# A last store in column pieces over all 128 rows, in a fused attention and GEGLU kernel

## The chip, the cores and the metric

The kernel runs on one core of a Trainium2 chip. The metric is the time of one execution on the device in microseconds; the figure for a kernel is the median of its runs. Traces come from one profiled execution, and times inside it count from the start of its span.

## What is computed

Squared-ReLU attention without a softmax, whose heads are joined to token rows, followed by a gated feed-forward block. The inputs are float32; `q`, `k` and `v` have the shape (8, 12, 448, 64), and the output has 3584 rows (8 batches of 448 tokens) of 768 columns.

```python
scores = scale * np.matmul(q, k.transpose(0, 1, 3, 2))     # scale = 1 / sqrt(64)
attn = np.maximum(scores, 0.0) ** 2 / S                    # S = 448
x = np.matmul(attn, v)                                     # heads joined: (3584, 768)
g = x @ w_gate                                             # (3584, 1536)
gelu = 0.5 * g * (1.0 + erf(g * inv_sqrt2))
val = x @ w_val
return (gelu * val @ w_out).astype(np.float32)             # (3584, 768)
```

## The kernel before

**Layout of the tokens.** The 448 tokens of a batch are seen as 64 positions times 7 chunks (P = 64, SC = 7): token 7p + c is position p of chunk c. A chunk is thus every seventh row of the output, and two neighbouring chunks lie one row apart. In DRAM a row of the output has 768 float32, 3072 bytes; two positions of one chunk are 7 rows apart.

**Stages.** Queries, keys and values are loaded and turned to bfloat16 by GpSimd's transfers, transposed, multiplied on TensorE as 64 by 64 blocks, passed through ReLU on ScalarE (line 740) and squared on VectorE (line 749). The value products give xT, the gate and value products with GELU give uT, and the output product makes rows of 768 columns. All matmuls go through the helper at line 406.

**The output product.** Tokens are taken in 14 groups (gr = 0 to 13, the last is FINAL) of four chunks. A group is two tiles, t0 and t1, of two chunks each, 128 rows with one chunk on partitions 0 to 63 and the next on 64 to 127 (HALF names the two halves). In the last group these are chunks 3 and 4, and 5 and 6, of the last batch. The product of a group is formed by seven smaller products, named 1 to 7 and taken in the order of CHAIN = "1726453". Each gives a 128 by 384 block (OGS = 384), the left or the right half of the columns of t0 or t1; some are added to a block already there. So each tile has its left and right half finished at different times, and the very last product is "3", the right half of t0.

**Around the change.** In `add_product`, `emit_read` (lines 1226 to 1232) takes a finished block out of PSUM into the tile `osb` in SBUF: a copy by ScalarE or VectorE (line 1231), or an addition by VectorE (line 1229). For the last group's "3" the copy is ScalarE's alone (`rd.other = None`). `emit_store` (lines 1247 to 1250) stores one half of the partitions, 64 rows of one chunk, as one transfer. A finished tile is usually stored by two such transfers of 192 KB over whole rows, on SP's queue; in the last two groups the second goes to ScalarE's queue. Tile t0 of the last group is the exception: its left and right columns are stored separately, each by two transfers of 96 KB, one half of the partitions on SP's queue and the other on ScalarE's. In every plain load and store, the 64 or 128 partitions are the outermost count of the transfer on both sides (lines 447, 456, 469, 485, 1250).

**Order of the work.** The kernel is written as operations with an engine, an estimated cost, dependencies and a priority (`Op`). `run_plan` emits them one after another in the order of a planned timetable: it takes at each step the operation that can start first, and at equal times the one with the lower `prio`. The order of the later TensorE units is a list written out by hand (LINE). The order of emission is each engine's program order; the waits between engines follow from what the instructions read and write. At the end of the program (line 1513) SP waits for the landing of every transfer, and the engines meet once more.

Of the kernel before, what the change touches and what calls it, by code (L numbers as in the profile page):

```python
# [316 lines left out]
def kernel(  # L317
# [10 lines left out]
    nc = tc.nc  # L328
# [5 lines left out]
    B, H, S, D = q.shape  # L334
    P = 64
    SC = S // P
# [13 lines left out]
    OGS = d_model // NG  # L350
# [62 lines left out]
    ACT, DVE, POOL, SP, IDLE = [], [], [], [], []  # L413
# [687 lines left out]
    sums, osb, stored = {}, {}, {}  # L1101
# [58 lines left out]
    def add_product(at, gr, name, final):  # L1160
# [4 lines left out]
        t0, t1 = 2 * gr, 2 * gr + 1  # L1165
        chunks = st["chunks"]
# [6 lines left out]
        box = st["box", stage]  # L1173
# [13 lines left out]
        else:  # L1187
            t, half = source
# [4 lines left out]
        def emit(r, fc):  # L1193
# [4 lines left out]
            for j in range(2):  # L1198
# [15 lines left out]
                for fc in range(KH)] for r in range(2)]  # L1214
        st["last", name] = ops[1][-1]
        left, right = slice(0, OGS), slice(OGS, 2 * OGS)
        t, cols, added = {"1": (t0, left, False), "2": (t0, left, True), "3": (t0, right, False),
                          "6": (t1, left, False), "4": (t1, left, True),
                          "7": (t1, right, False), "5": (t1, right, True)}[name]

        def osb_of(t):
            if t not in osb:
                osb[t] = opool.tile([TT, d_model], f32, name="osb", tag="osb")
            return osb[t]

        def emit_read(copy=nc.scalar.copy):
            o = osb_of(t)[:, cols]
            if added:
                ins = nc.vector.tensor_tensor(o, box[0][:, 0:OGS], o, op=ALU.add)
            else:  # L1230
                ins = copy(o, box[0][:, 0:OGS])  # L1231
            rd.ins = ins.ins

        engine = "DVE" if added else "ACT"
        before = {"2": "1", "4": "6", "5": "7"}.get(name)
        rd = Op(engine, 0.52 if added else 0.45, emit_read,
                [ops[1][-1], *([st["read", before]] if before else ())], lag=0.2, prio=0,
                other=None if added else ("DVE", 0.52, lambda: emit_read(nc.vector.tensor_copy)))
        if not added:
            rd.takes = osb_ring, lambda: stored[t][-1] if t in stored else None, t  # L1240
        reads = [rd]
        if final and name == "3":
            rd.other = None
        (DVE if added else ACT).append(rd)
        st["read", name] = rd
        st["read", stage] = rd
        def emit_store(j, engine=nc.sync, part=slice(0, d_model)):
            b, c = chunks[t % 2][j]
            rows = out[b * S:(b + 1) * S, :].rearrange("(p c) d -> c p d", c=SC)
            engine.dma_start(rows[c, :, part], osb[t][HALF[j], part])  # L1250

        if name in "2345":
            st["done", t] = [*st.get(("done", t), ()), *reads]
            if final and t == t0:
                SP.append(Op("SP", 0.6, lambda: emit_store(0, nc.sync, cols), reads, prio=-1))
                ACT.append(Op("ACT", 0.5, lambda: emit_store(1, nc.scalar, cols), reads, prio=-1))
                SP[-1].stored = ACT[-1].stored = 0.25
            elif len(st["done", t]) == 2:
                queues = (SP, "SP", 0.6, nc.sync), (ACT, "ACT", 0.5, nc.scalar)
                stored[t] = []  # L1260
                for j in range(2):
                    pool, name_, cost, engine = queues[j if gr >= FINAL - 1 else 0]
                    op = Op(name_, cost, lambda j=j, engine=engine: emit_store(j, engine), st["done", t],
                            lag=2.5, prio=-1)
                    op.stored = 0.5
                    stored[t].append(op)
                    pool.append(op)
# [83 lines left out]
    for gr in range(FINAL + 1):  # L1351
        work += [(LATER, 5, add_product, (gr, x, gr == FINAL)) for x in CHAIN]
# [47 lines left out]
    for kind, lo, hi in pairs:  # L1400
        if kind == "with":
            upper.append((tau[place[lo]], hi))
        else:
# [8 lines left out]
            t = tau[min(behind + 1, len(PE0))]  # L1412
# [47 lines left out]
    for u in later:  # L1460
        if u.name[0] == "o":
            b = u.name[1]
# [55 lines left out]
```

## Time and profile before

| | us |
|---|---|
| median of 3 runs | 403.87 (403.24 to 403.89) |
| the profiled execution, its own time | 404.06 |
| its span, first to last instruction | 402.3 |
| granted TensorE clock, mean | 0.996 |
| ScalarE busy (61%) | 243.6 |
| DMA traffic of the queues | 44.38 MB |

The span is what the trace can explain; the execution has some 1.8 us around it. Engines have short names in the rows: PE is TensorE's matmul, PEld its weight load, DVE VectorE, ACT ScalarE, POOL GpSimd, SP SyncE. A name with a q (SPq, ACTq) is the engine's sequencer: it issues transfers and waits, which is not counted as busy. Of DMA, the share is the mean busy share of the core's 16 DMA engines; q1 is the queue on which SP issues, q10 that of ScalarE, q0 that of GpSimd. A transfer is listed as issued, with its size and the time from issue to landing. In a row of instructions, `128x384 f32<-128x384 f32` is the output's and the input's shape, `x34` the count, and behind the bar stand busy microseconds and the mean nanoseconds of one.

### The profile page before, as it was taken

The page shows a single profiled execution, that of the slowest core. Times are in us where ns is not written, and L with a number is a line of the kernel's source. Part 1 is how long each engine was busy: PE and PEld are TensorE (multiplying, and loading weights), DVE is VectorE, ACT ScalarE, POOL GpSimd, SP SyncE. Part 2 cuts the span into 40 slices and gives each one's busy share as a digit, 9 for nine tenths or more (in the row PEclk, how much of TensorE's full clock was granted, in tenths as well). Part 3 has the DMA queues.
Part 4 walks back from the last instruction along what each step waited for, and adds up shares of the span by engine and source line. Part 5 has one row for each costly group of instructions (what it writes and reads, how often), then busy time and mean ns, then how long its engine had stood idle before and what let it go on. Part 6 is the DMA issues. An engine that isn't in the chain of part 4 may idle for free.

```text
span 402.3 us, 18625 instructions
## 1 busy us (share of the span) xinstructions
PE 393.5 (98%) x8510; PEld 339.5 (84%) x8510; DVE 301.5 (75%) x518; ACT 243.6 (61%) x362; POOL 76.8 (19%) x124
## 2 busy tenths in 40 slices
PE   8999999999999999999999999999999999999994
PEld 3555888888999979999999989768998899998884
DVE  2886886558878877898998787779888875786642
ACT  4957777376677667766767666556766535353130
POOL 6548323160320402101210303010110000000000
PEclk9999999999999999999999999999999999999998
DMA  7999999699696886755758988463542320000244
GB/s 104 175 185 165 196 197 155 95 161 151 100 216 91 141 196 91 112 68 86 89 97 190 162 132 124 95 108 51 57 56 70 95 68 4 2 3 3 58 125 137
DMA packets 75022, 44.38 MB, mean 110 GB/s; under 512 B 34368, under 2 KB 71488, under 8 KB 74944
## 3 DMA queue, kind: packets, MB, share of 16 engines
q0 software_dynamic: 38752, 24.39, 44.7%
q1 hardware_dynamic: 35792, 18.03, 22.2%
q8 instruction: 66, 1.08, 1.1%
q10 hardware_dynamic: 400, 0.79, 0.6%
q14 instruction: 12, 0.10, 0.1%
HBM read 48.76 MB, written 11.01 MB: 149 GB/s over the span
## 4 chain that ended last, share of the span: by engine, by line
PE 98%; issue 1%; ACT 0%; DVE 0%
PE ff L406 85%; PE sp L406 9%; PE ff L594 1%; PE sp L673 1%; PE ff L1425 1%; PE ff L673 1%; PE ff L636 0%; ACT attnT L740 0%; ACT qkT L644 0%; ACT osb L1231 0%; DVE held L392 0%; DVE table L395 0%; ACT xT L822 0%
## 5 line engine op out<-in xcount | busy, mean ns | idle before, releaser
L406 PE MATMUL ff<-xT,wg 64*64 64x448 bf16 x1872 | 189.6, 349 | 0.5 <-issue 0.5
L740 ACT ACTIVATE attnT<-sp 128x896 bf16<-128x896 f32 x168 | 151.3, 921 | 54.1 <-PE sp L406 46.0
L406 PE MATMUL ff<-xT,wv 64*64 64x448 bf16 x1440 | 153.1, 349 | 0.5 <-issue 0.5
L406 PEld LDWEIGHTS <-wv 64*64 64x64 bf16 x1872 | 111.1, 106 | 13.2 <-issue 2.3
L406 PEld LDWEIGHTS <-wg 64*64 64x64 bf16 x1872 | 110.7, 106 | 10.8 <-issue 0.4
L749 DVE TENSOR_TENSOR attnT<-attnT 128x1792 bf16<-128x1792 bf16 (+1 forms) x98 | 92.3, 954 | 10.9 <-ACT attnT L740 10.5
L406 PE MATMUL ff<-attnT,v 64*64 64x448 bf16 (+1 forms) x768 | 84.8, 326 | 0.3 <-issue 0.2
L406 PEld LDWEIGHTS <-s 64*64 64x64 bf16 x1344 | 77.3, 107 | 4.2 <-issue 0.2
L406 PE MATMUL sp<-qkT 64*64 64x448 bf16 (+1 forms) x768 | 79.3, 328 | 1.0 <-ACT qkT L644 0.6
L406 PE MATMUL ff<-wo,s 64*64 64x384 bf16 x672 | 59.6, 323 | 0.0
L406 PEld LDWEIGHTS <-uT 64*64 64x64 bf16 x912 | 54.8, 107 | 2.4
L1039 DVE TENSOR_TENSOR uT<-gel,ff 128x448 bf16<-128x448 bf16 x60 | 37.1, 619 | 21.9 <-PE ff L406 19.4
L406 PE MATMUL ff<-wt,s 64*64 64x384 bf16 x672 | 52.8, 322 | 0.0
L406 PEld LDWEIGHTS <-v 64*64 64x64 bf16 x768 | 47.4, 107 | 4.7 <-issue 1.5
L406 PE MATMUL ff<-ts,ws 64*64 64x448 bf16 x432 | 50.0, 349 | 0.0
L406 PE MATMUL ff<-ts,wv 64*64 64x448 bf16 x432 | 49.6, 349 | 0.0
L483 POOL DMA_DIRECT2D v<-in_v_dram x48 | 29.7, 632 | 89.1 <-ACT attnT L740 49.2
L406 PE MATMUL ff<-wo,uT 64*64 64x384 bf16 x576 | 46.4, 322 | 0.0
L406 PEld LDWEIGHTS <-qkT 64*64 64x64 bf16 x768 | 38.6, 106 | 8.5 <-issue 4.4
L1034 ACT ACTIVATE gel<-ff 128x448 bf16<-128x448 f32 x60 | 32.7, 546 | 21.1 <-PE ff L406 20.7
L406 PEld LDWEIGHTS <-ws 64*64 64x64 bf16 x648 | 39.8, 106 | 3.2
L956 DVE TENSOR_TENSOR part<-ff,part 128x448 f32<-128x448 f32 x54 | 32.6, 622 | 8.2 <-PE ff L406 6.0
(60 smaller groups left out, 381.8 us busy)
## 6 DMA issues: line engine op xcount, KB each, us to landing
out_dram<-osb SPq DMA_DIRECT2D x51, 192.0 KB, 3.4
v<-in_v_dram POOLq DMA_DIRECT2D x48, 128.0 KB, 5.0
qk<-in_q_dram POOLq DMA_DIRECT2D x23, 224.0 KB, 4.9
qk<-in_k_dram POOLq DMA_DIRECT2D x23, 224.0 KB, 5.5
wg<-in_moe_w_gate_dram POOLq DMA_DIRECT2D x6, 384.0 KB, 8.6
wv<-in_moe_w_val_dram POOLq DMA_DIRECT2D x6, 384.0 KB, 9.8
wo<-in_moe_w_out_dram POOLq DMA_DIRECT2D x8, 288.0 KB, 9.3
out_dram<-osb ACTq DMA_DIRECT2D x3, 192.0 KB, 3.3
```

The source lines that it names most:

```text
L406: return nc.tensor.matmul(o, lhsT, rhs, start=start, stop=stop, skip_group_check=onto, tile_position=(P * row, P * col))
L483: return nc.gpsimd.dma_start(v16[b, m][HALF[i], :, :, :], v[b, h0:h1].rearrange("h (p c) d -> p h c d", c=SC)[:, :, c0:c0 + VC, :])
L594: nc.tensor.matmul(t[:, :], warm[:, 0:128], warm[:, :], start=True, stop=True)
L673: nc.tensor.transpose(t[HALF[j], c, :], src[:, 2 * r + j, c, :], ident[:, :], tile_position=(0, P * j))
L740: relu.ins = nc.scalar.activation(duo["a"][:, u % 2, :, :], box[0][:, :, 0:S], AF.Relu).ins
L749: nc.vector.tensor_tensor(a[:, part], a[:, part], a[:, part], op=ALU.mult)
L956: rd.ins = nc.vector.tensor_tensor(t[:, :], box[0][:, 0:S], t[:, :], op=ALU.add).ins
L1034: nc.scalar.activation(gel[b, fc][:, :], box[0][:, 0:S], AF.Gelu)
L1039: u_op[b, fc].ins = nc.vector.tensor_tensor(uT[b][:, fc, :], gel.pop((b, fc))[:, :], box[0][:, 0:S], op=ALU.mult).ins
L1425: nc.tensor.matmul(t[HALF[j], :], warm[:, HALF[j]], warm[:, :], start=True, stop=True, tile_position=(0, P * j))
```

## The change

It touches product "3" of the last group, the right half of t0. Its copy of 384 columns by ScalarE becomes two copies of 192 columns, one after the other. Each piece is stored by one transfer over all 128 rows: the first on SP's queue, waiting for the first copy, the second on ScalarE's queue, waiting for the second. Before, the two transfers waited for the whole copy and each took 64 rows of all 384 columns. The DRAM side of the new transfers is `rows[c:c + 2]`, a view with two chunks, 64 positions and 192 columns; the SBUF side is 128 partitions by 192 columns. The planner's costs of the copies are 0.32 each.

```diff
         if final and name == "3":
-            rd.other = None
+            half = OGS // 2
+            copies = []
+
+            def emit_piece(h):
+                part = slice(OGS + h * half, OGS + (h + 1) * half)
+                ins = nc.scalar.copy(osb_of(t)[:, part], box[0][:, h * half:(h + 1) * half])
+                copies.append(ins)
+                if h == 0:
+                    rd.ins = ins.ins
+                return ins
+
+            rd.other, rd.cost, rd.emit = None, 0.32, lambda: emit_piece(0)
+            reads.append(Op("ACT", 0.32, lambda: emit_piece(1), [rd], lag=0.2, prio=-2))
+            reads[1].after = rd
+            ACT.append(reads[1])
+
+        def emit_wide(h, engine):
+            part = slice(OGS + h * OGS // 2, OGS + (h + 1) * OGS // 2)
+            (b, c), (b_, c_) = chunks[t % 2]
+            assert b == b_ and c_ == c + 1
+            rows = out[b * S:(b + 1) * S, part].rearrange("(p c) d -> c p d", c=SC)
+            engine.dma_start(rows[c:c + 2], osb[t][:, part])
...
-            if final and t == t0:
+            if final and t == t0 and name == "3":
+                SP.append(Op("SP", 0.6, lambda: emit_wide(0, nc.sync), [rd], prio=-1))
+                ACT.append(Op("ACT", 0.5, lambda: emit_wide(1, nc.scalar), [reads[1]], prio=-1))
+                SP[-1].stored = ACT[-1].stored = 0.25
+            elif final and t == t0:
                 SP.append(Op("SP", 0.6, lambda: emit_store(0, nc.sync, cols), reads, prio=-1))
```

## The prediction, made before the change was run

> **What bounds the kernel now.** I read the page first, then the chain of work that ended last over the final microseconds, then the instructions, the transfers and SP's waits after the last matmul.
>
> ```profile
> span 402.3 us, 18625 instructions
> PE 393.5 (98%) x8510; PEld 339.5 (84%) x8510; DVE 301.5 (75%) x518; ACT 243.6 (61%) x362; POOL 76.8 (19%) x124
> ```
>
> TensorE is busy for 98% of the span, so only two things can move the time: TensorE's own work, or what remains to be done when it has finished. The diff leaves the matmuls alone. The chain over 390 to 403 us shows where they end:
>
> ```profile
> 389.99 7.27 PE ff L406 x157
> 397.25 0.02 issue
> 397.27 0.48 ACT osb L1231
> ```
>
> The last matmul ends at 397.25, and ScalarE's copy of the last product runs to 397.75. The span ends at 402.3, so the **tail** is 5.05 us, and 4.5 us of it lie behind the copy. The last issue in ScalarE's timeline, and the transfers issued between 397.2 and 398.4 with their microseconds to landing, fill it:
>
> ```profile
> 397.78 0.50 ACTq L1250 DMA_DIRECT2D out_dram<-osb  x1
> ...
> out_dram<-osb ACTq DMA_DIRECT2D x1, 192.0 KB, 3.8
> out_dram<-osb SPq DMA_DIRECT2D x1, 96.0 KB, 3.1
> out_dram<-osb ACTq DMA_DIRECT2D x1, 96.0 KB, 3.3
> ```
>
> Two 96 KB stores are issued at 397.78, one on SP's queue and one on ScalarE's. They land 3.1 and 3.3 us later, the last at about 401.06. From there to 402.3 the program only closes (1.24 us): SP's waits on line 1513.
>
> ```profile
> SPq L1513 <- DMA out_dram<-osb: 2.6, 2, 2.3
> ```
>
> So the landing of the very last store sets the end. How the 3.3 us are spent is read from the busy share of the 16 DMA engines; the last two columns are that share and GB/s:
>
> ```profile
> 397.75:398.25 0.50, 0.00 (x0) 0.00 (x0) 0.00 (x0) 0.00 (x1) 0.00 (x0) 1.00 0.82 264
> 398.25:398.75 0.50, 0.00 (x0) 0.00 (x0) 0.00 (x0) 0.00 (x0) 0.00 (x0) 1.00 0.99 344
> 398.75:399.25 0.50, 0.00 (x0) 0.00 (x0) 0.00 (x0) 0.00 (x0) 0.00 (x0) 0.75 0.96 326
> 399.25:399.75 0.50, 0.00 (x0) 0.00 (x0) 0.00 (x0) 0.00 (x0) 0.00 (x0) 0.50 0.89 295
> 399.75:400.25 0.50, 0.00 (x0) 0.00 (x0) 0.00 (x0) 0.00 (x0) 0.00 (x0) 0.50 0.92 335
> 400.25:400.75 0.50, 0.00 (x0) 0.00 (x0) 0.00 (x0) 0.00 (x0) 0.00 (x0) 0.50 0.12 40
> ```
>
> All 16 engines are nearly full until 400.25, on stores of the preceding products and then on these two. The 0.12 in the last row is 0.06 us per engine, so an engine ends on average at 400.31. The landing at 401.06 comes 0.75 us later: part is the slowest engine's lag, part the way home. The tail is therefore bound by **DMA engine time**, and what the change does to that decides.
>
> **The change, part by part.** *The copies.* One copy of 384 columns becomes two of 192, a shape that the trace does not have. The copies of 384 and 448 columns, by form, are nearest, and the pair of copies at 389.29 shows how two follow each other:
>
> ```profile
> L952 ACT COPY part<-ff 128x448 f32<-128x448 f32 x35 | 18.5, 533 | 18.6 <-PE ff L406 16.1 <-DVE uT L965 1.8
> L1231 ACT COPY osb<-ff 128x384 f32<-128x384 f32 x34 | 16.2, 479 | 24.6 <-PE ff L406 23.4 <-issue 1.1
> ...
> 389.29 0.86 ACT L1231 COPY osb<-ff 128x384 f32<-128x384 f32 x2 [1.54 <-PE ff L406]
> ```
>
> 64 columns are worth 533 - 479 = 54 ns, so 192 columns less are worth 162, and a piece takes 479 - 162 = 317 ns (nothing saved, 479, is one end; half of it, 240, the other). Two copies took 0.86 us instead of 0.96, so the second starts 0.10 before the first ends. The first piece is done at 397.27 + 0.32 = 397.59, 0.16 earlier than now; the second at 397.59 - 0.10 + 0.32 = 397.81, 0.06 later. SP's store goes out 0.16 earlier and ScalarE's 0.06 later. Behind SP's store only the closing waits are queued, behind ScalarE's only its closing drain; TensorE and VectorE have nothing left. The planner places the new copy after everything else, so nothing ahead of 397.25 moves. Were SP's store held until the second copy too, it would go out at 397.84, which costs it 0.22; with the engines full until 400.25 either start disappears in their backlog.
>
> *The stores.* Before, a transfer carries 64 rows of 1536 bytes; after, 128 rows of 768 bytes. The bytes are the same. What matters is among how many engines the rows are dealt.
>
> ```profile
> q10 hardware_dynamic: 400, 0.79, 0.6%
> ...
> out_dram<-osb ACTq DMA_DIRECT2D x3, 192.0 KB, 3.3
> ...
> out_dram<-osb ACTq DMA_DIRECT2D x2, 96.0 KB, 2.8
> ```
>
> ScalarE's queue, q10, carries exactly five stores, and 400 packets are 80 for each: 64 rows and 16 short ones. I read this as sixteen equal shares of four rows, each with a closing packet. Every plain load and store of this kernel (lines 447, 456, 469, 485 and 1250) has 64 or 128 as the outermost count on both sides, and 16 divides both. The new transfer is the first that has not: in DRAM its rows are `c p d` with c = 2 outermost, p = 64 inside, since the rows of one chunk lie 21.5 KB apart and the two chunks 3 KB apart, so that no single count of 128 describes them. The SBUF side has 128. If the shares are cut along the outermost count, as all shares here can have been, there are **two**: one engine takes the 64 rows of the first chunk, one those of the second, and fourteen do nothing. Both stores are cut alike, so I let both have the same pair. No row shows such a transfer. Sixteen shares would need a cut inside the inner count on one side and in the outer one on the other; nothing in the trace needs that. I take two.
>
> The Trainium skill, page "DMA: Bandwidth & Descriptors", section "Why a DMA increments its semaphore by 16 and not by 1", states the same: the engine count is the largest up to 16 that divides the slowest dimension of both sides, on these queues the lowest-numbered engines. By that rule the count here is 2, and both stores share one pair; the trace's 16 short packets per 64-row store agree, and no run yet shows a smaller count.
>
> *The price of a row.* Two windows hold one whole store of ScalarE's queue each, 389.9 to 390.6 (96 KB) and 395.95 to 396.66 (192 KB); a third, 180.7 to 180.9, only 256-byte packets of the transposing transfers:
>
> ```profile
> q10 hardware_dynamic: 80, 0.10, 41.0%
> ...
> q10 hardware_dynamic: 80, 0.20, 70.5%
> ...
> DMA packets 168, 0.04 MB, mean 215 GB/s; under 512 B 168, under 2 KB 168, under 8 KB 168
> ## 3 DMA queue, kind: packets, MB, share of 16 engines
> q1 hardware_dynamic: 168, 0.04, 106.7%
> ```
>
> Engine time is share x window x 16: 0.410 x 0.70 x 16 = 4.59 us, 72 ns per row of 1536 bytes with the short packets in it; 0.705 x 0.71 x 16 = 8.01 us, 125 ns per row of 3072; 1.067 x 0.20 x 16 / 168 = 20 ns per 256 bytes. On the line from 20 to 72, 768 bytes cost 20 + 52 x 512/1280 = 41 ns; I take 40, as the 72 include the short packets. The ends are 20 and 72.
>
> *The sum.* Now each engine spends 2 x 4.59/16 = 0.57 us on the two stores. With two shares on one pair, each of the two engines has 2 x 64 x 40 ns = 5.12 us of them, 4.55 more. It ends at 400.31 + 4.55 = 404.86. Of the 0.75 us above I keep 0.4 for the way home and drop 0.35 as the lag among sixteen engines, which two hardly have (an estimate); so the last store lands at 405.26 instead of 401.06: **+4.2 us**. The closing 1.24 us stays. The profiled execution took 404.06 us, 402.3 of it span; the median of the runs is 403.87. So I forecast 408.26 for the former and 403.87 + 4.2, rounded, 408.1 for the median. With 20 ns a row the sum is 2.56 - 0.57 - 0.35 = +1.6 (405.5), with 72 it is 9.2 - 0.57 - 0.35 = +8.3 (412.2).
>
> **The rivals.** *Sixteen shares, engines bind: no change.* If the rows are dealt over all engines whatever the outermost count, each has 16 x 40 = 0.64 us instead of 0.57. SP's half starts 0.16 earlier, ScalarE's 0.06 later, and the end moves by between -0.05 and +0.15 us: about 403.9. For it: the bytes are the same and every store so far ran on sixteen. Against it: none of them had a small outermost count. It decides as soon as the engine count does not depend on that count. The Trainium skill, the same page, section "Rules for kernel authors", advises one 128-partition transfer instead of two over disjoint halves, because halves share the same engines anyway; by that advice alone the result is this rival's, and the trace agrees only in that both stores now overlap on full engines.
>
> *Dealt better than feared.* Either sixteen shares with a pace set by the number of rows, or two stores on different pairs. Two stores alone in the window 304.5 to 307.5 show the pace:
>
> ```profile
> DMA  0000000000000007985976948996299695952000
> ```
>
> Busy in 22 of 40 slices of 75 ns, 1.65 us for 128 rows, though two stores of 8.01 us need only 1.0 on sixteen engines. At that pace 128 more rows add up to 1.65 us. Different pairs give 64 x 40 ns = 2.56 - 0.57 - 0.35 = +1.6. Both end near 405.5. Against the first: the engines' shares above leave no room for a slower feeder in the tail; against the second: nothing in the text of the transfers tells one queue's engines from the other's.
>
> *A gain.* If the tail hung on the first store's start, 0.16 us could be won; that is within what a measurement can tell from no change (0.2%, 0.8 us), so faster by more needs something that I cannot name.
>
> **How the numbers follow.** Two shares on one pair 0.75, dealt better 0.10, no change 0.13, faster 0.02. The first two are slower by over 0.2% (0.85), the third is within it. Within the forecast most lies between 406.3 and 410.5, as 72 ns is the price of a row twice as long. The range runs from 405.0, which takes in the second case, to 410.5; outside are no change (0.13), faster (0.02) and a long row's price (about 0.04).
>
> **What would show it.** The same engines' shares, after the last matmul: near 2/16 = 0.12 for some 4 us after 400.3, at 40 GB/s or so, would show two engines; a fall to zero at 400.5 would show sixteen. Packets on q10 should be 64 + 16 for each old store and 128 and some short ones for the new one, 2 short if there are two shares. ScalarE should have one copy more, of 0.32 us, and its store issue near 397.84; SP's wait for the last transfer should grow from 2.3 to about 6.5 us. A landing about 3.3 us after issue would prove the forecast wrong, and so would a change ahead of 397.25.

## The result, and the profile after

The changed kernel takes 408.5 us in the median (407.71 to 409.19), beside 403.56 us for the kernel before (401.56 to 403.89), four runs each. The ratio is 1.0123, with a 95% interval of 1.009 to 1.0156: slower by 1.2%. The profiled execution took 408.88 us, 4.82 more than that of before. From its page come the span and the packets of ScalarE's queue:

```profile
span 407.1 us, 18624 instructions
...
q10 hardware_dynamic: 450, 0.79, 0.6%
```

The queue carried 400 packets before. Four of its five stores are the old ones with 80 packets, 320 in all; so the new one has 130: 128 rows and **two** short packets, where every store of this queue had sixteen. The chain that ended last, over 390 to 408 us, shows that little moved ahead of the stores:

```profile
389.97 7.58 PE ff L406 x161
397.55 0.02 issue
397.57 0.06 ACT osb L1248
397.63 0.16 issue
397.79 0.32 ACT osb L1248
```

The last matmul ends at 397.55, 0.30 later than in the profiled execution of before, and the span ends at 407.1. I call the time from the end of the last matmul to the end of the span the **tail**: 5.04 us before, 9.54 after, by the times of the trace (the rows are rounded). The two copies stand where they were expected. The timelines of ScalarE and of SP go on:

```profile
397.57 0.54 ACT L1248 COPY osb<-ff 128x192 f32<-128x192 f32 x2 [5.58 <-PE ff L406]
398.14 1.21 ACTq L1264 DMA_DIRECT2D out_dram<-osb  x1
```

```profile
397.92 0.62 SPq L1264 DMA_DIRECT2D out_dram<-osb  x1
```

What fills the tail is again read from the stretches of half a microsecond; the last two columns are the busy share of 16 DMA engines and GB/s:

```profile
399.75:400.25 0.50, 0.00 (x0) 0.00 (x0) 0.00 (x0) 0.00 (x0) 0.00 (x0) 0.71 0.39 118
400.25:400.75 0.50, 0.00 (x0) 0.00 (x0) 0.00 (x0) 0.00 (x0) 0.00 (x0) 0.50 0.14 29
400.75:401.25 0.50, 0.00 (x0) 0.00 (x0) 0.00 (x0) 0.00 (x0) 0.00 (x0) 0.50 0.12 29
401.25:401.75 0.50, 0.00 (x0) 0.00 (x0) 0.00 (x0) 0.00 (x0) 0.00 (x0) 0.50 0.11 32
...
402.25:402.75 0.50, 0.00 (x0) 0.00 (x0) 0.00 (x0) 0.00 (x0) 0.00 (x0) 0.50 0.14 46
...
403.75:404.25 0.50, 0.00 (x0) 0.00 (x0) 0.00 (x0) 0.00 (x0) 0.00 (x0) 0.50 0.14 46
404.25:404.75 0.50, 0.00 (x0) 0.00 (x0) 0.00 (x0) 0.00 (x0) 0.00 (x0) 0.50 0.11 37
404.75:405.25 0.50, 0.00 (x0) 0.00 (x0) 0.00 (x0) 0.00 (x0) 0.00 (x0) 0.50 0.07 23
405.25:405.75 0.50, 0.00 (x0) 0.00 (x0) 0.00 (x0) 0.00 (x0) 0.00 (x0) 0.50 0.05 15
```

Before, the share stood at 0.92 until 400.25 and then fell to nothing. Now it drops to 0.14, which is two of sixteen engines (2/16 = 0.125, and packets overlap a little), and stays at 0.11 to 0.14 for more than 4 us; from 404.75 it is 0.07, one engine. At 46 GB/s the pair moves 23 GB/s each, one row of 768 bytes in 33 ns. That pace holds from 402.25 on; in the stretches before it the pair is about as busy but moves only 29 to 41 GB/s, which the experiments come back to. SP's waits at the end of the program are now

```profile
SPq L1538 <- DMA out_dram<-osb: 7.1, 3, 4.5
```

against 2.6 us before. The last store lands at 405.91, and the program closes.

### The profile page after: what moved, and what is told of

It reads as the page before. It is cut to its first block, busy times and chain, and to the rows that moved or that the text cites. A ratio compares the mean times of both kernels' runs of the same rounds, so it can differ in the third digit from the quotient of the medians.

```text
span 407.1 us, 18624 instructions
## 1 busy us (share of the span) xinstructions
PE 391.6 (96%) x8507; PEld 338.5 (83%) x8510; DVE 301.8 (74%) x518; ACT 243.8 (60%) x363; POOL 76.9 (19%) x124
## 4 chain that ended last, share of the span: by engine, by line
PE 93%; DMA 3%; POOL 1%; issue 1%; ACT 0%; SPq 0%; POOLq 0%
PE ff L406 83%; PE sp L406 8%; DMA qk<-in_k_dram 2%; DMA qkT<-qkr 1%; PE sp L673 1%; POOL qk L468 1%; PE ff L594 1%; PE ff L673 1%; ACT attnT L740 0%; ACT osb L1248 0%; POOL ident masks.py:199 0%; POOL ident masks.py:197 0%; SPq L515 0%; ACT xT L822 0%; POOLq L1527 0%
## 5 line engine op out<-in xcount | busy, mean ns | idle before, releaser
L406 PEld LDWEIGHTS <-wg 64*64 64x64 bf16 x1872 | 108.4, 106 | 10.7
L749 DVE TENSOR_TENSOR attnT<-attnT 128x1792 bf16<-128x1792 bf16 (+1 forms) x98 | 92.3, 953 | 10.8 <-ACT attnT L740 10.3
L406 PE MATMUL sp<-qkT 64*64 64x448 bf16 (+1 forms) x768 | 75.9, 328 | 3.0 <-DMA qkT<-qkr 1.7
L406 PEld LDWEIGHTS <-s 64*64 64x64 bf16 x1344 | 74.4, 107 | 4.8 <-issue 0.2
L406 PEld LDWEIGHTS <-uT 64*64 64x64 bf16 x912 | 52.4, 107 | 2.9
L406 PEld LDWEIGHTS <-v 64*64 64x64 bf16 x768 | 46.5, 107 | 5.0 <-issue 1.9
L406 PEld LDWEIGHTS <-qkT 64*64 64x64 bf16 x768 | 36.5, 106 | 10.4 <-issue 3.9
```

Source lines behind the costliest of these rows:

```text
L406: return nc.tensor.matmul(o, lhsT, rhs, start=start, stop=stop, skip_group_check=onto, tile_position=(P * row, P * col))
L749: nc.vector.tensor_tensor(a[:, part], a[:, part], a[:, part], op=ALU.mult)
```

## The experiments

Theory: shares are cut along the outermost count, here 2, and the tail is the time of the engines that get a share. Rivals: short rows (128 rows of 768 bytes are slow wherever they go), copies and issue, the spacing of the rows in DRAM, a fixed delay of such transfers. The time of an execution varies by a few microseconds with where the last matmul ends (395.0 to 398.7 in these profiles, with the same matmuls, but for one kernel that stands still in the middle), so the tail tells more than one run's time. Each tail is that of one profiled execution; where ratios are given they rest on several runs.

**Only the outermost count is changed.** The wide stores go to the rows of the first batch, as N blocks of 128/N neighbouring rows, and the right columns of the last t0 are left unwritten; copies, number of issues, bytes and rows per transfer stay. (In the edit N stands for the number of blocks: the run with N = 2 has `n=2` and `0:64`.)

```diff
-            rows = out[b * S:(b + 1) * S, part].rearrange("(p c) d -> c p d", c=SC)
-            engine.dma_start(rows[c:c + 2], osb[t][:, part])
+            rows = out[0:S, part].rearrange("(n r) d -> n r d", n=N)[:, 0:128 // N, :]
+            engine.dma_start(rows, osb[t][:, part])
```

N = 2:

> The two wide stores go to other rows, in the first batch (stored long before), as 2 blocks of 64 neighbouring rows: outermost count 2 as in the changed kernel, another spacing of the rows. It leaves the right rows of the last product unwritten. The tail is the time from the end of the last matmul to the end of the span: 5.05 us before, 9.5 after. Theory (shares are cut along the outermost count, here 2, and the two engines' time is the tail): tail 9.5 us, 2 completions. Rival 'spacing' (rows 21.5 KB apart in two chunks 3 KB apart collide in memory): the tail falls to 5 to 6 us. Rival 'short rows' (128 rows of 768 bytes are slow whatever the engines): 9.5.

N = 4:

> As blocks2, but 4 blocks of 32 rows, so an outermost count of 4; same rows, bytes, copies and issues. The last product's right rows stay unwritten. Theory: four engines with 2 x 32 rows each, half the time of the pair, so of the 4.5 us lost about 2.4 come back: tail 6.7 to 7.2 us. Rival 'short rows' and rival 'copies and issue' (the second copy and the later issues): 9.5 us.

N = 16:

> As blocks2, but 16 blocks of 8 rows, an outermost count of 16. The last product's right rows stay unwritten. Theory: sixteen engines with 16 rows each, 0.64 us: tail 5.0 to 5.4 us, median within 0.5 us of the kernel before. Rival 'short rows' and rival 'copies and issue': tail 9.5 us, median 408 to 409.

N = 8, after the first three:

> As blocks2, blocks4 and blocks16, with 8 blocks of 16 rows, an outermost count of 8; the last product's right rows stay unwritten. Theory: eight engines with 2 x 16 rows, 1.06 us each: tail 5.4 to 6.2 us if all engines start together; blocks4 (8.97 instead of 6.7 to 7.2) had one engine some 1.65 us behind the three others, and such a laggard would make it 6.5 to 8.

N = 4 once more:

> blocks4 once more (the last product's right rows stay unwritten), since its tail of 8.97 us missed the 6.7 to 7.2 that four equal engines should give, with one engine 1.65 us behind. If the laggard is an accident of one execution: 6.7 to 7.4. If it belongs to the kernel: 8.5 to 9.3, with one late completion again.

The span and the packets of ScalarE's queue, from the pages with N = 2, 4, 8 and 16 in turn:

```profile
span 405.8 us, 18624 instructions
...
q10 hardware_dynamic: 450, 0.79, 0.6%
```

```profile
span 404.5 us, 18624 instructions
...
q10 hardware_dynamic: 452, 0.79, 0.6%
```

```profile
span 404.7 us, 18624 instructions
...
q10 hardware_dynamic: 456, 0.79, 0.6%
```

```profile
span 403.8 us, 18624 instructions
...
q10 hardware_dynamic: 464, 0.79, 0.6%
```

Less 320 for the four old stores and 128 for the rows, these are 2, 4, 8 and 16 short packets: one for each share. The chain has the end of the last matmul, here for N = 2 and then for N = 16; span less this is the tail:

```profile
396.02 0.02 issue
```

```profile
398.75 0.02 issue
```

| N | rows on one engine | at 33 ns | tail, us | over 5.04 |
|---|---|---|---|---|
| 2 | 128 | 4.2 | 9.78 | 4.74 |
| 4 | 64 | 2.1 | 8.97, again 8.78 | 3.93, 3.74 |
| 8 | 32 | 1.1 | 6.34 | 1.30 |
| 16 | 16 | 0.5 | 5.02 | none |

With an outermost count of 16, everything else as in the changed kernel, the loss is gone; the ratio to the kernel before is 0.9993 (0.9956 to 1.003). So it is neither the short rows, nor the copies, nor the number of issues. With N = 2 the rows have another spacing and the loss stays, so the spacing is not it. N = 4 **missed** the 6.7 to 7.2 of equal engines in both executions (the second time within the 8.5 to 9.3 that was named for a lasting laggard), and N = 8, at 6.34, came out between the 5.4 to 6.2 of equal engines and the 6.5 to 8 with a laggard: there is a second term that the number of rows doesn't give. The stretches of N = 4 show where it sits:

```profile
398.50:399.00 0.50, 0.00 (x0) 0.00 (x0) 0.00 (x0) 0.00 (x0) 0.00 (x0) 0.50 0.11 5
...
400.50:401.00 0.50, 0.00 (x0) 0.00 (x0) 0.00 (x0) 0.00 (x0) 0.00 (x0) 0.50 0.21 72
401.00:401.50 0.50, 0.00 (x0) 0.00 (x0) 0.00 (x0) 0.00 (x0) 0.00 (x0) 0.50 0.15 49
401.50:402.00 0.50, 0.00 (x0) 0.00 (x0) 0.00 (x0) 0.00 (x0) 0.00 (x0) 0.50 0.07 23
402.00:402.50 0.50, 0.00 (x0) 0.00 (x0) 0.00 (x0) 0.00 (x0) 0.00 (x0) 0.50 0.07 23
402.50:403.00 0.50, 0.00 (x0) 0.00 (x0) 0.00 (x0) 0.00 (x0) 0.00 (x0) 0.50 0.07 23
```

Three engines are done by about 401.5, and one works on alone (0.07, 23 GB/s) for 1.5 us more. Such a laggard came in both executions: the trace has a completion event for each engine of a store, and the last of the four came 0.77 and 1.65 us after the third for the two stores, and 1.18 and 1.20 the second time. The first row shows something else: early on the busy engines hardly moved anything (5 GB/s).

**The same pieces in transfers of 64 rows.**

```diff
-                SP.append(Op("SP", 0.6, lambda: emit_wide(0, nc.sync), [rd], prio=-1))
-                ACT.append(Op("ACT", 0.5, lambda: emit_wide(1, nc.scalar), [reads[1]], prio=-1))
-                SP[-1].stored = ACT[-1].stored = 0.25
+                for j in range(2):
+                    SP.append(Op("SP", 0.6, lambda j=j: emit_store(j, nc.sync, slice(OGS, OGS + OGS // 2)),
+                                 [rd], prio=-1))
+                    SP[-1].stored = 0.12
+                for j in range(2):
+                    ACT.append(Op("ACT", 0.5, lambda j=j: emit_store(j, nc.scalar, slice(OGS + OGS // 2, 2 * OGS)),
+                                  [reads[1]], prio=-1))
+                    ACT[-1].stored = 0.12
```

> The two column copies stay, but each piece is stored by two transfers of 64 rows (one chunk each), outermost count 64: both of the first piece on SP's queue, both of the second on ScalarE's. Rows of 768 bytes as in the changed kernel, 256 of them. Theory: 16 shares each, tail 5.1 to 5.7 us (the second issue on each queue comes 0.5 us later than a single one), median within 0.8 us of the kernel before. Rival 'short rows': 9.5 us.

Its page has the span, its chain the end of the last matmul:

```profile
span 403.1 us, 18626 instructions
```

```profile
398.13 0.02 issue
```

The tail is 4.98 us, a little under the 5.1 to 5.7 that was expected, the ratio 1.0002 (0.9972 to 1.0031). The 256 rows of 768 bytes are all there, now with the outermost count 64, and cost nothing; nor do two more issues show. This is the column split as such, with its early first piece, and it brings nothing that can be measured.

**The copies alone**, with the stores of before, which wait for both pieces:

```diff
-            if final and t == t0 and name == "3":
-                SP.append(Op("SP", 0.6, lambda: emit_wide(0, nc.sync), [rd], prio=-1))
-                ACT.append(Op("ACT", 0.5, lambda: emit_wide(1, nc.scalar), [reads[1]], prio=-1))
-                SP[-1].stored = ACT[-1].stored = 0.25
-            elif final and t == t0:
+            if final and t == t0:
```

> Only the copy is cut into two column pieces; the stores are the old ones, 64 rows of 384 columns each, waiting for both copies. Theory: the second piece ends 0.06 us later than the one copy did, so the tail (end of the last matmul to end of the span; 5.04 us before) is 5.0 to 5.2 us and the median stays within noise. Rival 'copies and issue': 9 us or more.

The tail was 5.03 us, the ratio 0.999 (0.9961 to 1.0019). The rival of copies and issue is out.

**One wide store and two narrow ones**: the first piece is stored as in the changed kernel, the second by two transfers of 64 rows.

```diff
-                ACT.append(Op("ACT", 0.5, lambda: emit_wide(1, nc.scalar), [reads[1]], prio=-1))
-                SP[-1].stored = ACT[-1].stored = 0.25
+                SP[-1].stored = 0.25
+                for j in range(2):
+                    ACT.append(Op("ACT", 0.5, lambda j=j: emit_store(j, nc.scalar, slice(OGS + OGS // 2, 2 * OGS)),
+                                  [reads[1]], prio=-1))
+                    ACT[-1].stored = 0.12
```

> The first piece is stored as in the changed kernel (128 rows, outermost count 2, SP's queue), the second by two transfers of 64 rows on ScalarE's queue. Theory with the 33 ns per row that the changed kernel shows on one engine: the pair has 64 rows each instead of 128, 2.1 us instead of 4.2, so the tail is 6.9 to 7.6 us. Rival 'a fixed delay': a transfer with a small outermost count is late by a fixed time, whatever its size: 9 to 9.8 us, as with two of them.

The tail was 8.20 us: above the theory, below the fixed delay. The two completions of the wide store came 1.40 us apart; without that gap the tail would be 8.20 - 1.40 = 6.8, near the theory. (The very last landing, 0.18 us later, is one of the sixteen shares of the second 64-row store.) So there is a term for the rows and one for a laggard.

**One copy, one wide store** of 384 columns on SP's queue:

```diff
+        def emit_wide(engine):
+            (b, c), (b_, c_) = chunks[t % 2]
+            rows = out[b * S:(b + 1) * S, cols].rearrange("(p c) d -> c p d", c=SC)
+            engine.dma_start(rows[c:c + 2], osb[t][:, cols])
...
-            if final and t == t0:
+            if final and t == t0 and name == "3":
+                SP.append(Op("SP", 0.6, lambda: emit_wide(nc.sync), reads, prio=-1))
+                SP[-1].stored = 0.5
+            elif final and t == t0:
```

> One copy of 384 columns as before, then one store of all 128 rows (1536 bytes each) on SP's queue, outermost count 2; no transfer on ScalarE's queue for this product. Theory if an engine's time goes with the bytes: 64 rows of 61 to 66 ns on each of two engines, 4.1 us, tail 8.8 to 9.6 us, median 407.5 to 408.5. If it goes with the number of rows (33 ns each whatever the length): 2.1 us, tail 6.9 to 7.6. Rival 'copies and issue' (no second copy, one issue): near 5 us.

The median was 408.44 us, the ratio 1.0162 (1.0126 to 1.0197), the tail 9.62, just past what the theory allows. The stretches:

```profile
400.50:401.00 0.50, 0.00 (x0) 0.00 (x0) 0.00 (x0) 0.00 (x0) 0.00 (x0) 0.50 0.14 52
...
402.50:403.00 0.50, 0.00 (x0) 0.00 (x0) 0.00 (x0) 0.00 (x0) 0.00 (x0) 0.50 0.07 28
403.00:403.50 0.50, 0.00 (x0) 0.00 (x0) 0.00 (x0) 0.00 (x0) 0.00 (x0) 0.50 0.07 25
```

One engine alone moves some 25 GB/s (the last two rows), and its last packets start 61 ns apart, beside 33 for rows of half the length: an engine's time goes with the bytes, and the number of rows hardly matters. With a single issue and the old copy the loss is all there. The completions are 1.06 us apart.

**Is the second engine slow, or hindered?** Two more kernels ask for the laggard. The first stores five tiles in the middle of the kernel (groups 7 to 9) by one transfer of 128 whole rows, and leaves the end as it was:

```diff
+            elif len(st["done", t]) == 2 and gr in (7, 8, 9) and chunks[t % 2][0][0] == chunks[t % 2][1][0]:
+                def emit_wide():
+                    b, c = chunks[t % 2][0]
+                    rows = out[b * S:(b + 1) * S, :].rearrange("(p c) d -> c p d", c=SC)
+                    nc.sync.dma_start(rows[c:c + 2], osb[t][:, :])
+                op = Op("SP", 0.6, emit_wide, st["done", t], lag=2.5, prio=-1)
...
```

> The kernel before, but the tiles of groups 7, 8 and 9 whose two chunks are in one batch are stored by one transfer of 128 whole rows, outermost count 2, on SP's queue, in the middle of the kernel where TensorE has work for long after; the last groups are as before. Theory: two engines, 64 rows of about 121 ns each, so each lands 8.5 to 10 us after its issue instead of 2.7, and the median stays the same, since nothing waits for it. About the second engine, which in the tails of the changed kernel and of one_wide lagged by 1.0 to 1.25 us: if traffic in the tail did that, the two completions come within 0.3 us of each other here; if the second engine is slower by itself, 1 us or more apart.

The first two, issued at 302.30 and 306.78, completed at 312.64 on both engines and at 320.17 and 320.18: no laggard. The other three ended 0.53, 0.40 and 0.41 us apart, between the two answers that were named. Even the first, which had the pair to itself, landed 10.3 us after its issue, not 8.5 to 10. The rest of what was expected **failed**: the median is 414.98 us, the ratio 1.0301 (1.0274 to 1.0328). The waits, and VectorE's timeline, say why:

```profile
PE ff L406 <- DVE osb L1231: 7.1, 1, 7.1
```

```profile
320.27 1.02 DVE L1231 COPY osb<-ff 128x384 f32<-128x384 f32 x2 [7.57 <-DMA out_dram<-osb]
```

The second store stood behind the first on the same two engines and landed 13.4 us after its issue; the copy that needed its `osb` buffer again waited, the product's bank was not freed, and TensorE stood still for 7.1 us. The page of this kernel has

```profile
span 413.3 us, 18619 instructions
PE 397.0 (96%) x8507; PEld 345.2 (84%) x8510; DVE 300.0 (73%) x515; ACT 245.6 (59%) x365; POOL 77.0 (19%) x124
```

Outside its busy time TensorE had 8.8 us before (402.3 - 393.5) and has 16.3 here, 7.5 more; the other 3.5 us of the longer span are more busy time for the same matmuls. The granted clock was down beside the stall (0.74 and 0.58 in the two stretches of 5 us after 315):

```profile
315.00:320.00 5.00, 0.00 (x0) 0.00 (x0) 0.00 (x0) 0.00 (x0) 0.00 (x0) 0.74 0.12 50
320.00:325.00 5.00, 4.12 (x62) 3.10 (x65) 2.49 (x4) 0.48 (x1) 0.00 (x0) 0.58 0.01 3
```

The second kernel takes older stores out of the end. As a measure, first that edit to the kernel before:

```diff
-            if final and t == t0:
+            if gr >= FINAL - 1 and t == t0:
```

> The kernel before, with the first tile of the last group but one (t0 of group 12) stored in column halves too: its left half goes out when product 2 of that group is done, so that only 192 KB instead of 384 KB of it are left for the last two microseconds. By the engine times of the kernel before that takes 2 x (8.01 - 4.59)/16 = 0.43 us of engine time out of the backlog, so the tail would be 4.6 to 5.05 us instead of 5.04 and the median 0 to 0.4 us lower (within what is measurable, or just). If the tail hangs on the way home of the last store alone, nothing changes.

The tail is 4.45 us in its profile, shorter than the 4.6 to 5.05 that was expected, but the median of 12 runs is 402.72 beside 402.55 (ratio 0.9999, 0.9979 to 1.0018): the 0.6 us, 0.15%, could not be told from no change, so no faster kernel is claimed. Then the same edit on the changed kernel:

```diff
-            elif final and t == t0:
+            elif gr >= FINAL - 1 and t == t0:
```

> The changed kernel, with the first tile of the last group but one stored in column halves as in split12, so that 192 KB less of older stores stand before the two wide ones. In the changed kernel the two engines' completions lie 1.25 and 1.02 us apart; in wide_quiet, where nothing else was in flight, 0.00 and 0.01. If the older stores in flight make the second engine late: completions at most 0.7 us apart and a tail of 8.2 to 9.0 us instead of 9.54. If the lag has another cause that goes with the end of the program: 1.0 to 1.3 us apart, tail 9.0 to 9.5 us (the 0.6 us that split12 won on sixteen engines may come off).

```profile
401.00:401.50 0.50, 0.00 (x0) 0.00 (x0) 0.00 (x0) 0.00 (x0) 0.00 (x0) 0.50 0.14 46
401.50:402.00 0.50, 0.00 (x0) 0.00 (x0) 0.00 (x0) 0.00 (x0) 0.00 (x0) 0.50 0.14 48
402.00:402.50 0.50, 0.00 (x0) 0.00 (x0) 0.00 (x0) 0.00 (x0) 0.00 (x0) 0.50 0.04 14
```

The share stays at 0.14 until 402.00; the stretch of one engine alone is gone. The completions are 0.39 and 0.07 us apart, and the tail is 8.60, that is 4.15 over split12 (one execution of each). All this is what was named for older stores in flight that make one engine late. Yet the excess over the kernel without wide stores hardly fell (4.15, beside 4.50 in the changed kernel), and the start and duration of each packet, which the rows above add up, tell more.

In the changed kernel one engine of the pair starts a row every 33 ns from 400.22 on. The other begins at 400.32, and seven of its first 15 rows last 138 to 193 ns instead of 36: those 15 take until 401.94, 1.6 us instead of 0.5. After that both keep the same pace. So the lag of some 1.1 us is lost in a few slow rows at the start of the wide stores; neither engine is slower by itself. With less backlog there are slow rows too, of up to 188 ns, but on both engines, and some as late as 398.65 to 399.57, though the last older store had landed at 397.58:

```profile
398.50:399.00 0.50, 0.00 (x0) 0.00 (x0) 0.00 (x0) 0.00 (x0) 0.00 (x0) 1.00 0.12 32
399.00:399.50 0.50, 0.00 (x0) 0.00 (x0) 0.00 (x0) 0.00 (x0) 0.00 (x0) 0.77 0.13 34
```

Each engine needed 5.1 to 5.4 us from its first wide row to its last, where 128 rows at 33 ns are 4.2. In the middle of the other kernel, where nothing older was in flight, the pair was busy from the start of the first wide store, but moved little at first:

```profile
304.50:305.50 1.00, 1.00 (x32) 0.87 (x27) 0.41 (x1) 0.55 (x1) 0.00 (x0) 1.00 0.11 31
...
306.50:307.50 1.00, 1.00 (x35) 0.92 (x31) 1.00 (x5) 0.82 (x2) 0.00 (x0) 1.00 0.12 49
```

Six rows on each engine took 180 to 544 ns instead of 121, at the same moments, so both lost 1.2 us and ended together. The second store, whose rows followed without a pause, had none. So completions that come together do not mean that nothing was lost, and slow rows do not need older stores in flight. The second term is the time that these rows cost; what makes them slow, and why one engine alone has them in the changed kernel, is open.

## Why the prediction was right, point by point

**The place.** Of the 4.82 us between the two profiled executions 4.50 lie in the tail. Another 0.30 is the later end of the last matmul; a change ahead of it was named as a sign of being wrong, but 0.30 is small beside the 395.0 to 398.7 over which that end is spread. The medians lie 4.9 us apart, where 4.2 were forecast. That the last landing sets the end, and that DMA engine time fills it, held.

**The copies.** A piece was put at 317 ns, their overlap at 0.10 us; the trace has 319 and 324 ns and the second starts 0.216 us after the first, an overlap of 0.10. Counted from the end of the last matmul, SP's issue came 0.16 us earlier and ScalarE's 0.06 later, as worked out, and neither shows in the tail.

**Two shares.** This was the choice on which the sign hung, and it held: two short packets, a share of 0.11 to 0.14, and with N = 4, 8 and 16 as many shares as the outermost count. The Trainium skill's rule for the number of engines (page "DMA: Bandwidth & Descriptors", section "Why a DMA increments its semaphore by 16 and not by 1") gives 2, 4, 8 and 16 for these; the traces agree with each. (Among these four only the DRAM side's count differs.) The Trainium skill's advice of one 128-partition transfer (the same page, section "Rules for kernel authors") would have given the first rival; here the wide transfers cost nothing with an outermost count of 16 (blocks16) and lost with 2, 4 and 8.

**The price of a row** was mis-sized: 40 ns were taken, 33 measured at 46 GB/s. 128 rows are 4.22 us, not 5.12, which is 0.9 less.

**The lag** was wrong in sign. The prediction dropped 0.35 us "as the lag among sixteen engines, which two hardly have". The two had more: 1.25 us between the completions of SP's store and 1.02 between those of ScalarE's, lost in slow rows that the prediction had no term for. With engine time of 4.22 - 0.57 = 3.65 more, the measured 4.50 leaves +0.85 where -0.35 stood. The two errors, -0.9 and +1.2, nearly cancel by luck, so 408.1 for a measured 408.5 looks better than its terms are.

**The rivals.** No change: it needed sixteen shares, and blocks16 and narrow show that it would have come true with them (5.02 and 4.98 us). A pace set by the rows fell with blocks16, which has the same 256 rows. Different pairs fell with the share, which never rose above 0.14 after 400.25. Of the signs that were named one came out otherwise: SP's longest wait is 4.5 and not about 6.5 us, because the wait falls into three parts (the last older store, the first wide one, the second), 7.1 us together.

## What to carry to other kernels

Before two transfers are made one, look at the outermost count: with 2 on the DRAM side, 96 KB that sixteen engines shared take the time of 48 KB on each of two, and the last store of a program has nothing to hide behind. Read it off the trace: the short packets per transfer, and the busy share of the engines, 2/16, tell how many take part. A slow store in the middle is not free either, since it holds its buffer, and whoever needs the buffer next waits.

## What the runs showed of the hardware that I had not expected

- An engine alone moves 23 GB/s in rows of 768 bytes and 25 in rows of 1536 (33 and 61 ns a row); where sixteen shared the work, their rows of 1536 bytes cost 72 ns with all that belongs to them.
- The issue itself grew: 0.62 us on SP and 1.21 on ScalarE for the wide stores, against 0.47 and 0.50. With N = 16 it was 0.59 on both. Behind them nothing waited.
- With two or four shares one engine ended 0.8 to 1.65 us after the others in the tail, and at most 0.4 us after them with 192 KB less of older stores, when both had lost time.
- In the first microseconds of a wide store some rows took about five times as long as later ones (up to 193 ns instead of 36 in the changed kernel, up to 544 instead of 121 for the rows of 3072 bytes), with older stores in flight and without.
